# A depthwise convolution and a gated feed-forward: inputs cast to bf16 by POOL's DMA queue in place of fp32 tiles and casts on the engines

## The chip, the cores and the metric

The kernel runs on one core of a Trainium2 chip. The metric is device microseconds of one execution. The median of three runs of the kernel before is 559.08 us (558.78 to 559.87); the execution that was profiled took 559.35 us.

## What is computed

The input `x` has 8 sequences of 3904 rows with 192 values (fp32). Each of 8 heads (24 columns) has 7 taps; their softmax is a causal convolution along the sequence, and its result, 31232 rows of 192, goes through a gated feed-forward with `d_ff` = 1024:

```
out[b, s, h, :] = sum over k of softmax(weight[h])[k] * x_pad[b, s + k, h, :]
y  = out.reshape(31232, 192)
return ((y @ w1) * (y @ w2)) @ w3 @ w_out
```

All inputs and the output are fp32.

## The kernel before

**Layout.** The rows are cut into two streams of 15616 (`NS = 2`), which ride together: partitions 0 to 63 hold stream 0, 64 to 127 stream 1. The convolution works on windows of 64 rows (58 new ones and 6 of history); 272 windows a stream are grouped in ten blocks of 10, 10, 10, 30, 32 and five times 36 windows (`SIZES`). The feed-forward works on chunks of 512 rows a stream, 31 of them (`NR`), the last of 256.

**Convolution.** `load_x` (L91) brings a block's windows into fp32 tiles `xr` (two buffers; blocks 0 to 2 take one tile, the others two halves). The loads go out on SP's DMA queue, a few on ACT's; each is 64 partitions by so many windows of 192 values, so each contiguous run is 768 bytes. `cast_x` (L127) zeroes the history rows at the start of a sequence with memsets on POOL, waits for the loads and casts the tile to bf16 (`xb`, two buffers), on POOL but for half of block 0 (ACT). `conv` (L246) multiplies with a banded 64 x 64 matrix of taps (`Aband`, made by `band_taps` and `band_sum`, L216 to L230, from masks that POOL makes at L174) and evicts into `convo` on ACT and DVE. `store` (L277) writes `convo` to the scratch `rows` in DRAM by SP's queue; `transposes` (L316) brings it back by DMA transposes as `xT`, three tiles that hold a ring of four chunks. The first blocks go another way: `pe_transposes` (L301) makes `xT` on TensorE, with copies on DVE and ACT.

**Feed-forward.** `first_product` (L344) makes `pa` and `pb` for eight tiles `ft` of `d_ff`, with two sets of weights (`wn` as loaded, `wsw`, printed as `ws`, with the halves of 64 partitions swapped), ACT copies `pa` to `asb` and DVE multiplies into `abT`. The weights `w1`, `w2` are loaded as fp32 (`wf`, L160) in two halves of 512 columns; `cast_w` (L332) casts each half to `wn` on POOL and to `wsw` on DVE, ACT and POOL. `w3` and `w_out` are loaded by POOL's queue with the cast to bf16 on the way (L396, L400) and multiplied once into `W_sb` (L402 to L417). `second_product` (L369) multiplies `abT` with `W_sb`, ACT copies to `osb` (a ring of six `slot` buffers, which `wf` and the band's products share) and SP's queue writes the output.

**Order.** Nothing is rescheduled: each engine and each queue works in the order in which the program names its instructions. The prologue (L422 to L472) names loads, casts, first convolutions, chunks 0 to 2 of the first product with blocks 1 to 3 of the convolution between their tiles, and the product of `w3` and `w_out`. Then a loop over R (L484) takes in each round the first product of chunk R, the second of chunk R - 2, some heads of the next block's convolution (`plan`), after a block's last head its store and the cast of the next block, the transposes of chunk R + 2, and, where a block's first head was among the heads, the loads of the block after it.

Of the kernel before, what the change touches and what calls it, by code (L numbers as in the profile page):

```python
# [9 lines left out]
FP32 = mybir.dt.float32  # L10
BF16 = mybir.dt.bfloat16
# [6 lines left out]
def kernel(  # L18
# [10 lines left out]
    nc = tc.nc  # L29
# [6 lines left out]
    PAD = K - 1  # L36
# [35 lines left out]
        return psum.tile([128, 16, 128], BF16, tag="banks", name=name)  # L72

    def slot(shape, dtype, name):
        return stage.tile(shape, dtype, tag="slot", bufs=6, name=name)

    rows = dram.tile([TS, NP * NS * Q], BF16, name="rows")

# [3 lines left out]
        return [(FIRST[b], 2 * n)] if 2 * n <= MAXN else [(FIRST[b], n), (FIRST[b] + n, n)]  # L82

    x_rows = x.rearrange("b s d -> (b s) d")
    xr_of, xb_of, zero_rows = {}, {}, {}

    def x_window(r, i, m):
        return bass.AP(tensor=x.tensor, offset=(r * TS + tok(i) - PAD) * D,
                       ap=[[D, Q], [ST * D, m], [1, D]])

    def load_x(b, q1=nc.sync):  # L91
        tiles = []
        zeros_of = zero_rows[b] = []
        for i0, n in halves_of(b):
            xr = work.tile([128, n, D], FP32, tag="xr", bufs=2, name="xr")
            w = 0
            if i0 == 0:
                nc.gpsimd.memset(xr[0:32, 0, :], 0.0)
                for p0, p1 in ((PAD, PAD + 48), (PAD + 48, Q)):
                    nc.sync.dma_start(out=xr[p0:p1, 0, :], in_=x_rows[p0 - PAD:p1 - PAD, :])  # L100
                nc.sync.dma_start(out=xr[0:Q, 1:n, :], in_=x_window(0, 1, n - 1))
                q1.dma_start(out=xr[Q:128, :, :], in_=x_window(1, 0, n))
                zeros_of.append((xr, 1, 0))
                w = n
            while w < n:
                i = i0 + w
                m = min(n - w, WB - i % WB)
                at_end = i + m == NWIN
                if at_end:
                    m -= 1  # L110
                if m:
                    for r, q in ((0, nc.sync), (1, q1)):
                        q.dma_start(out=xr[Q * r:Q * r + Q, w:w + m, :], in_=x_window(r, i, m))
                if i % WB == 0:
                    zeros_of += [(xr, 0, w), (xr, 1, w)]
                w += m
                if at_end:
                    nc.gpsimd.memset(xr[Q:128, w, :], 0.0)
                    t = tok(NWIN - 1) - PAD
                    nc.sync.dma_start(out=xr[0:Q, w, :], in_=x_rows[t:t + Q, :])  # L120
                    nc.sync.dma_start(out=xr[Q:Q + PAD + LAST, w, :],
                                      in_=x_rows[TS + t:TS + t + PAD + LAST, :])
                    w += 1
            tiles.append(xr)
        xr_of[b] = tiles

    def cast_x(b, engines=None):  # L127
        tiles = []
        for xr, r, w in zero_rows.pop(b):
            nc.gpsimd.memset(xr[Q * r:Q * r + PAD, w, :], 0.0)  # L130
        for xr in xr_of.pop(b):
            n = xr.shape[1]
            xb = work.tile([128, n, D], BF16, tag="xb", bufs=2, name="xb")
            parts = engines or [nc.gpsimd.tensor_copy]
            step = -(-n // len(parts))
            for e, f in enumerate(parts):
                ws = slice(e * step, min(n, (e + 1) * step))
                f(out=xb[:, ws, :], in_=xr[:, ws, :])  # L138
            tiles.append(xb)
        if len(tiles) == 1:  # L140
            n = SIZES[b] // 2
            xb_of[b] = [(tiles[0], 0), (tiles[0], n)]
        else:
            xb_of[b] = [(tiles[0], 0), (tiles[1], 0)]


    wall = const.tile([128, H, K], FP32)
    nc.scalar.dma_start(out=wall, in_=weight.partition_broadcast(128))
    load_x(0, nc.scalar)

    tiny = const.tile([128, 1], FP32)
    nc.vector.memset(tiny, 0.0)
    zeros = const.tile([128, CH], BF16)
    nc.vector.memset(zeros, 0.0)  # L154
    nc.scalar.activation(out=tiny, in_=tiny, func=ACT.Exp)

    wf = [slot([128, DFF], FP32, f"wf{k}") for k in range(3)]
    HC = DFF // 2

    def load_w(half, q1):  # L160
        cs = slice(half * HC, (half + 1) * HC)
        nc.sync.dma_start(out=wf[0][:, cs], in_=moe_w1[0:128, cs])
        q1.dma_start(out=wf[1][:, cs], in_=moe_w2[0:128, cs])
        nc.sync.dma_start(out=wf[2][0:Q, cs], in_=moe_w1[128:192, cs])
        q1.dma_start(out=wf[2][Q:128, cs], in_=moe_w2[128:192, cs])

    load_w(0, nc.scalar)

    ones = const.tile([128, 1], BF16)
    nc.gpsimd.memset(ones, 1.0)  # L170
# [2 lines left out]
    for m, base in ((cmask, 0), (lmask, -Q)):  # L173
# [2 lines left out]
            pattern=[[-1, K], [-1, Q]], compare_op=ALU.is_equal,  # L176
            fill=0.0, base=base, channel_multiplier=1)
    nc.vector.tensor_copy(out=cmask[Q:128], in_=lmask[Q:128])
    ident = const.tile([128, 128], BF16)
    make_identity(nc, ident)  # L180

    def warm(n):
        t = banks("warm")
# [40 lines left out]
    def band_sum(g):  # L224
        with nc.allow_low_precision(reason="one tap and zeros"):
            nc.vector.reduce_sum(out=Aband[:, g, 0],
                                 in_=cprod_of.pop(g).rearrange("p h k s -> p h s k"),
                                 axis=AX.X)
        nc.vector.tensor_copy(out=Aband[Q:128, g, 1], in_=Aband[0:Q, g, 0])
        nc.scalar.copy(out=Aband[0:Q, g, 1], in_=Aband[Q:128, g, 0])  # L230
# [15 lines left out]
    def conv(b, h0, nh, evict=None):  # L246
        n = SIZES[b] // 2
        if h0 == 0:
            convo_of[b] = work.tile([128, n, NP, NS, Q], BF16, tag="convo", bufs=2, name="convo")
        convo = convo_of[b]  # L250
        cps = banks("cps")
        wd = nh * G

        def view(ps, r):
            return cps[ps, r, 0:n * wd].rearrange("p (w g) -> p w g", g=wd)

        for j in range(nh):
            h = h0 + j
            for c in range(2):
                xb, w0 = xb_of[b][c]  # L260
                for r in range(NS):
                    nc.tensor.matmul(  # L262
                        view(slice(Q * c, Q * c + Q), r)[:, :, j * G:(j + 1) * G],
                        band_of(h, r),
                        xb[Q * r:Q * r + Q, w0:w0 + n, h * G:(h + 1) * G],
                        start=True, stop=True)
        src = cps[:, :, 0:n * wd].rearrange("p r (w g) -> p r w g", g=wd)
        o = 0
        for e, (k, c0, m) in enumerate(segments(h0 * G, wd)):
            dst = convo[:, :, k, :, c0:c0 + m].rearrange("p w r g -> p r w g")  # L270
            f = evict or [nc.scalar.copy]
            f[e % len(f)](out=dst, in_=src[:, :, :, o:o + m])  # L272
            o += m
        if h0 + nh == H:
            del xb_of[b]
# [45 lines left out]
                out=xT[k][:, a:a + t1 - t0], in_=rows[t0:t1, k * 128:(k + 1) * 128])  # L321


    wn = [const.tile([128, DFF], BF16, name=f"wn{k}", tag=f"wn{k}") for k in range(3)]
    wsw = [const.tile([128, DFF], BF16, name=f"ws{k}", tag=f"ws{k}") for k in range(3)]

    def w_of(i, k, r):
        if k == 2:
            return (wn if i == r else wsw)[2]
        return (wn if k == r else wsw)[i]  # L330

    def cast_w(k, half, direct, swap):  # L332
        cs = slice(half * CH, (half + 1) * CH)
        direct(out=wn[k][:, cs], in_=wf[k][:, cs])
        for f, (d, s) in zip(swap, ((0, Q), (Q, 0))):
            f(out=wsw[k][d:d + Q, cs], in_=wf[k][s:s + Q, cs])  # L336


    abT_of = {}
# [79 lines left out]

    V, A, P = nc.vector.tensor_copy, nc.scalar.copy, nc.gpsimd.tensor_copy  # L420

    load_w(1, nc.sync)  # L422
    load_x(1)
    band_taps(0, nc.vector)
    band_taps(1, nc.gpsimd)
    cast_x(0, engines=(A, P))
    load_x(2, nc.scalar)
    band_sum(0)
    band_sum(1)
    conv(0, 0, 4)  # L430
    warm(3)
    cast_w(0, 0, P, (V, A))
    conv(0, 4, 4, evict=(V, A))
    cast_w(2, 0, P, (V, A))
    cast_w(1, 0, P, (P, P))
    pe_transposes(0)
    for k in (0, 2, 1):
        cast_w(k, 1, P, (P, A))
    cast_x(1)
    load_x(3)  # L440
    load_wo()
    for jt in range(2):
        load_w3(jt)
    cast_x(2)
    for jt in range(2, JT):
        load_w3(jt)

    def seq(*fs):
        def run():
# [6 lines left out]
        5: seq((conv, 1, 4, 4)),  # L456
        7: seq((pe_transposes, 1), (store, 1, 19), (conv, 2, 0, 4))})
    first_product(1, {
        0: seq((conv, 2, 4, 4), (cast_x, 3), (store, 2), (transposes, 2, 1152), (load_x, 4)),
        7: seq((conv, 3, 0, 1), (conv, 3, 1, 1))})  # L460
    first_product(2, {
        1: seq((conv, 3, 2, 1), (conv, 3, 3, 1)),
        3: seq((conv, 3, 4, 1), (conv, 3, 5, 1)),
        5: seq((conv, 3, 6, 1), (conv, 3, 7, 1), (store, 3), (transposes, 3), (transposes, 4))})

    cast_x(4)
    w3_transpose(0)
    w3_transpose(1)
    for jt in range(JT):
# [14 lines left out]
    for R in range(LAG, NR + LAG):  # L484
        if LAG < R < NR:
            first_product(R)
        for r in range(NS):
            second_product(R - LAG, r)
        heads = plan.get(R, [])
        for j, (b, h) in enumerate(heads):  # L490
            conv(b, h, 1, (V,) if j < 2 else (A,))
        if heads and heads[-1][1] == H - 1:
            store(b)
            if b + 1 < NB:
                cast_x(b + 1)
        if LAG < R < NR - 2:
            transposes(R + 2)
        if heads and heads[0][1] == 0 and b + 1 < NB:
            load_x(b + 1)


# [28 lines left out]
```

## Time and profile before

| what | value |
|---|---|
| profiled execution | 559.35 us |
| its span (first to last instruction of the profile) | 557.6 us |
| PE busy | 528.1 us (95%) |
| DVE, ACT, POOL busy | 356.3, 319.9, 64.5 us |
| SP's queue (q1) | 128294 packets, 73.16 MB |
| POOL's queue (q0) | 2192 packets, 2.49 MB |
| ACT's queue (q10) | 1680 packets, 1.41 MB |
| chain that ended last: PE, DMA, ACT, DVE | 87%, 5%, 3%, 2% |

How to read it: busy times are of one execution and overlap. The chain that ended last is followed back from the last instruction, at each step to what released it, and so says on what the end depended. A bracket behind a row of the timeline names the idle time of its engine before it and what ended it. "SPq" is SP's issuing of DMAs. Bytes are counted as written, so a cast from fp32 to bf16 counts half of what is read.

### The profile page before, as it was taken

How to read it: one execution, taken by the hardware profiler on the slowest of the kernel's cores; microseconds unless marked ns; L12 is line 12 of the kernel's file. 1: busy time of each engine (PE TensorE's matmuls, PEld its weight loads, DVE VectorE, ACT ScalarE, POOL GpSimd, SP SyncE). 2: the span in 40 equal slices, each digit the busy share in tenths (PEclk: the TensorE clock that was granted, in tenths of full speed). 3: DMA queues.
4: the chain of work that ended last, by engine and by line, in shares of the span. 5: the costliest groups of instructions: out<-in, count | busy, mean ns of one | idle time of the engine just before them, and what ended most of it. 6: DMA issues, size and time to landing. Idle time of an engine off the chain costs nothing.

```text
span 557.6 us, 12681 instructions
## 1 busy us (share of the span) xinstructions
PE 528.1 (95%) x5425; PEld 343.7 (62%) x5425; DVE 356.3 (64%) x329; ACT 319.9 (57%) x360; POOL 64.5 (12%) x56
## 2 busy tenths in 40 slices
PE   5892889999999999999999999999999999999997
PEld 2441367666566666566666666666655666665587
DVE  5573374667866667876666886666786655677640
ACT  2872645555665555665555665554666555566642
POOL 5733030013004000040000400021000000000000
PEclk8897799999999999999999999999999999999999
DMA  8898898957896899367982779827234462223214
GB/s 183 165 223 189 162 198 161 193 117 157 184 215 141 152 177 186 80 152 149 200 184 56 163 165 198 157 73 144 70 86 86 116 160 62 65 58 86 72 58 142
DMA packets 132222, 77.86 MB, mean 140 GB/s; under 512 B 49858, under 2 KB 130374, under 8 KB 132166
## 3 DMA queue, kind: packets, MB, share of 16 engines
q1 hardware_dynamic: 128294, 73.16, 62.3%
q0 software_dynamic: 2192, 2.49, 2.6%
q10 hardware_dynamic: 1680, 1.41, 1.2%
q8 instruction: 42, 0.69, 0.6%
q14 instruction: 14, 0.11, 0.1%
HBM read 33.29 MB, written 35.13 MB: 123 GB/s over the span
## 4 chain that ended last, share of the span: by engine, by line
PE 87%; DMA 5%; ACT 3%; DVE 2%; SPq 1%; issue 1%; ACTq 0%; POOL 0%; POOLq 0%
PE ops L375 28%; PE pa L357 28%; PE pb L357 27%; DMA xT<-rows 2%; PE cps L262 2%; ACT asb L363 2%; DMA xr<-in_x_dram 2%; DVE abT L364 1%; DMA rows<-convo 1%; PE wps L415 1%; ACT osb L380 1%; SPq L320 1%; PE w3ps L406 0%; PE tps L307 0%; ACT ws L336 0%
## 5 line engine op out<-in xcount | busy, mean ns | idle before, releaser
L364 DVE TENSOR_TENSOR abT<-asb,pb 128x1024 bf16<-128x1024 bf16 (+1 forms) x248 | 298.0, 1203 | 79.3 <-ACT asb L363 49.2
L363 ACT CAST asb<-pa 128x1024 bf16<-128x1024 f32 (+1 forms) x248 | 247.4, 999 | 75.0 <-PE pa L357 74.1
L357 PE MATMUL pa<-xT,wn 64*128 64x512 bf16 (+1 forms) x744 | 200.8, 374 | 4.9 <-DMA xT<-rows 1.4
L357 PE MATMUL pa<-xT,ws 64*128 64x512 bf16 (+1 forms) x744 | 200.9, 374 | 2.5 <-DMA xT<-rows 1.9
L357 PE MATMUL pb<-xT,wn 64*128 64x512 bf16 (+1 forms) x744 | 201.8, 374 | 0.7 <-DVE abT L364 0.7
L357 PE MATMUL pb<-xT,ws 64*128 64x512 bf16 (+1 forms) x744 | 195.3, 374 | 0.0
L357 PEld LDWEIGHTS <-wn 64*128 64x128 bf16 x1488 | 137.4, 94 | 91.5 <-issue 13.2
L357 PEld LDWEIGHTS <-ws 64*128 64x128 bf16 x1488 | 128.9, 94 | 74.0 <-issue 10.0
L375 PEld LDWEIGHTS <-abT 128*128 128x128 bf16 x1952 | 159.6, 98 | 11.7 <-issue 11.7
L375 PE MATMUL ops<-W_sb,abT 128*128 128x192 bf16 x1952 | 166.1, 246 | 0.0
L380 ACT COPY osb<-ops 128x768 f32<-128x768 f32 (+1 forms) x62 | 48.8, 788 | 127.7 <-PE ops L375 127.7
L272 DVE CAST convo<-cps 128x864 bf16<-128x864 f32 (+4 forms) x53 | 44.9, 894 | 95.4 <-PE cps L262 95.4
L138 POOL CAST xb<-xr 128x3456 bf16<-128x3456 f32 (+4 forms) x17 | 45.6, 2701 | 238.5 <-PE cps L262 155.5
L262 PE MATMUL cps<-xb,Aband 64*64 64x432 bf16 (+3 forms) x320 | 19.0, 320 | 15.2 <-POOL xb L138 9.9
L272 ACT CAST convo<-cps 128x640 bf16<-128x640 f32 (+8 forms) x29 | 15.3, 581 | 11.6 <-PE cps L262 10.7
L262 PEld LDWEIGHTS <-Aband 64*64 64x64 bf16 x320 | 6.5, 109 | 24.1 <-issue 21.4
L130 POOL MEMSET xr<- 6x192 f32 x7 | 1.7, 250 | 67.2 <-DMA xr<-in_x_dram 67.1
L185 PE MATMUL warm<-zeros 128*128 128x512 bf16 x19 | 8.0, 604 | 1.3 <-DVE zeros L154 1.3
L415 PE MATMUL wps<-wo_b,w3T 128*128 128x192 bf16 x64 | 6.6, 246 | 1.3 <-DVE w3T L409 1.2
L409 DVE COPY w3T<-w3ps 128x1024 bf16<-128x1024 bf16 x8 | 5.4, 689 | 2.9 <-PE w3ps L406 2.9
L417 ACT CAST W_sb<-wps 128x192 bf16<-128x192 f32 x8 | 2.5, 318 | 8.2 <-PE wps L415 8.2
L415 PEld LDWEIGHTS <-w3T 128*128 128x128 bf16 x64 | 5.1, 98 | 1.7 <-DVE w3T L409 1.7
(41 smaller groups left out, 50.9 us busy)
## 6 DMA issues: line engine op xcount, KB each, us to landing
out_dram<-osb SPq DMA_DIRECT2D x60, 384.0 KB
xr<-in_x_dram SPq DMA_DIRECT2D x14, 864.0 KB
rows<-convo SPq DMA_DIRECT2D x7, 648.0 KB
xr<-in_x_dram SPq DMA_DIRECT2D x4, 720.0 KB
xr<-in_x_dram SPq DMA_DIRECT2D x5, 480.0 KB
xr<-in_x_dram SPq DMA_DIRECT2D x6, 384.0 KB
w3b<-in_moe_w_dram POOLq DMA_DIRECT2D x8, 256.0 KB, 12.8
xr<-in_x_dram SPq DMA_DIRECT2D x2, 816.0 KB
```

The lines of the kernel that those rows point to most:

```text
L138: f(out=xb[:, ws, :], in_=xr[:, ws, :])
L185: nc.tensor.matmul(t[:, j % 2, :], zeros[:, 0:128], zeros, start=True, stop=True)
L262: nc.tensor.matmul(view(slice(Q * c, Q * c + Q), r)[:, :, j * G:(j + 1) * G], band_of(h, r), xb[Q * r:Q * r + Q, w0:w0 + n, h * G:(h + 1) ...
L272: f[e % len(f)](out=dst, in_=src[:, :, :, o:o + m])
L320: nc.sync.dma_start_transpose(out=xT[k][:, a:a + t1 - t0], in_=rows[t0:t1, k * 128:(k + 1) * 128])
L357: nc.tensor.matmul(p[:, r, 0:N], w_of(i, k, r)[rs, ft * 128:(ft + 1) * 128], xT[k][rs, r0:r0 + N], start=(k == 0), stop=(k == NP - 1))
L363: nc.scalar.copy(out=asb[:, :, 0:N], in_=pa[:, :, 0:N])
L364: nc.vector.tensor_tensor(out=ab[:, ft, :, 0:N], in0=asb[:, :, 0:N], in1=pb[:, :, 0:N], op=ALU.mult)
L375: nc.tensor.matmul(ops[:, g // 2, (g % 2) * D:(g % 2) * D + D], ab[:, jt, r, g * 128:(g + 1) * 128], W_sb[:, jt, :], start=(jt == 0), stop ...
L380: nc.scalar.copy(out=osb.rearrange("p (a g) d -> p a (g d)", g=2), in_=ops[:, 0:ng // 2, 0:2 * D])
L409: nc.vector.tensor_copy(out=w3T_of[jt], in_=tps[:, 0:JT, :])
L415: nc.tensor.matmul(wps[:, 0, 0:D], w3T[:, gt, :], wo_b[:, gt, :], start=(gt == 0), stop=(gt == JT - 1))
```

## The change

All of x and all weights of the first product go by POOL's queue (`nc.gpsimd.dma_start`) straight into bf16 tiles, the cast being made on the way. The fp32 tiles `xr` and `wf` and the casts `cast_x` and `cast_w` are gone; what stays of the latter is `swap_w`, which copies the halves of 64 partitions from `wn` to `wsw`. `xb` has six buffers in place of two, the `slot` ring five in place of six. The zero rows at the start of a sequence are set in `xb` just before the block's first convolution. In block 0 the first window is loaded apart (`load_first`), after the masks. Block 4 is loaded in the prologue after `w3`, and in the loop the next block's loads stand ahead of the heads of the block before.

```diff
     def slot(shape, dtype, name):
-        return stage.tile(shape, dtype, tag="slot", bufs=6, name=name)
+        return stage.tile(shape, dtype, tag="slot", bufs=5, name=name)
...
-    def load_x(b, q1=nc.sync):
+    def load_x(b):
...
-            xr = work.tile([128, n, D], FP32, tag="xr", bufs=2, name="xr")
+            xb = work.tile([128, n, D], BF16, tag="xb", bufs=6, name="xb")
...
+                nc.gpsimd.memset(xb[:, 0, :], 0.0)
+                for r in range(NS):
+                    nc.gpsimd.dma_start(out=xb[Q * r:Q * r + Q, 1:n, :], in_=x_spans(r, 1, n - 1))
...
-                    for r, q in ((0, nc.sync), (1, q1)):
-                        q.dma_start(out=xr[Q * r:Q * r + Q, w:w + m, :], in_=x_window(r, i, m))
+                    for r in range(NS):
+                        nc.gpsimd.dma_start(out=xb[Q * r:Q * r + Q, w:w + m, :],
+                                            in_=x_spans(r, i, m))
...
-    def cast_x(b, engines=None):
...
+    def load_first():
+        xb = xb_of[0][0][0]
+        for r in range(NS):
+            for p0, p1 in ((PAD, PAD + 48), (PAD + 48, Q)):
+                nc.gpsimd.dma_start(
+                    out=xb[Q * r + p0:Q * r + p1, 0, :],
+                    in_=x_rows[r * TS + p0 - PAD:r * TS + p1 - PAD, :])
...
-    load_x(0, nc.scalar)
+    load_x(0)
...
-    wf = [slot([128, DFF], FP32, f"wf{k}") for k in range(3)]
...
-    load_w(0, nc.scalar)
...
     nc.vector.tensor_copy(out=cmask[Q:128], in_=lmask[Q:128])
+    load_first()
     ident = const.tile([128, 128], BF16)
     make_identity(nc, ident)
+
+    wn = [const.tile([128, DFF], BF16, name=f"wn{k}", tag=f"wn{k}") for k in range(3)]
+    wsw = [const.tile([128, DFF], BF16, name=f"ws{k}", tag=f"ws{k}") for k in range(3)]
+    nc.gpsimd.dma_start(out=wn[0], in_=moe_w1[0:128, :])
+    nc.gpsimd.dma_start(out=wn[2][0:Q], in_=moe_w1[128:192, :])
+    nc.gpsimd.dma_start(out=wn[2][Q:128], in_=moe_w2[128:192, :])
...
-    def cast_w(k, half, direct, swap):
-        cs = slice(half * CH, (half + 1) * CH)
-        direct(out=wn[k][:, cs], in_=wf[k][:, cs])
-        for f, (d, s) in zip(swap, ((0, Q), (Q, 0))):
-            f(out=wsw[k][d:d + Q, cs], in_=wf[k][s:s + Q, cs])
+    def swap_w(k, half, engines):
+        cs = slice(half * HC, (half + 1) * HC)
+        for f, (d, e) in zip(engines, ((0, Q), (Q, 0))):
+            f(out=wsw[k][d:d + Q, cs], in_=wn[k][e:e + Q, cs])
...
-    load_w(1, nc.sync)
-    load_x(1)
     band_taps(0, nc.vector)
     band_taps(1, nc.gpsimd)
-    cast_x(0, engines=(A, P))
-    load_x(2, nc.scalar)
+    nc.gpsimd.dma_start(out=wn[1], in_=moe_w2[0:128, :])
+    for b in (1, 2):
+        load_x(b)
     band_sum(0)
+    conv(0, 0, 4)
     band_sum(1)
-    conv(0, 0, 4)
     warm(3)
-    cast_w(0, 0, P, (V, A))
+    swap_w(0, 0, (V, A))
     conv(0, 4, 4, evict=(V, A))
-    cast_w(2, 0, P, (V, A))
-    cast_w(1, 0, P, (P, P))
+    swap_w(2, 0, (V, A))
+    swap_w(1, 0, (V, A))
     pe_transposes(0)
     for k in (0, 2, 1):
-        cast_w(k, 1, P, (P, A))
-    cast_x(1)
+        swap_w(k, 1, (P, A))
     load_x(3)
     load_wo()
-    for jt in range(2):
+    for jt in range(JT):
         load_w3(jt)
-    cast_x(2)
-    for jt in range(2, JT):
-        load_w3(jt)
+    load_x(4)
...
-        0: seq((conv, 2, 4, 4), (cast_x, 3), (store, 2), (transposes, 2, 1152), (load_x, 4)),
+        0: seq((conv, 2, 4, 4), (store, 2), (transposes, 2, 1152)),
...
-    cast_x(4)
...
         heads = plan.get(R, [])
+        if heads and heads[0][1] == 0:
+            b = heads[0][0]
+            for xb, r, w in zero_rows.pop(b):
+                nc.gpsimd.memset(xb[Q * r:Q * r + PAD, w, :], 0.0)
+            if b + 1 < NB:
+                load_x(b + 1)
         for j, (b, h) in enumerate(heads):
             conv(b, h, 1, (V,) if j < 2 else (A,))
         if heads and heads[-1][1] == H - 1:
             store(b)
-            if b + 1 < NB:
-                cast_x(b + 1)
         if LAG < R < NR - 2:
             transposes(R + 2)
-        if heads and heads[0][1] == 0 and b + 1 < NB:
-            load_x(b + 1)
```

Each engine's own work keeps its order: PE's instructions are the same, one for one, in the same order as before.

More of the change, by code (lines that the diff above doesn't have):

```diff
@@ L84, with x_spans @@
     x_rows = x.rearrange("b s d -> (b s) d")
-    xr_of, xb_of, zero_rows = {}, {}, {}
-    def x_window(r, i, m):
+    xb_of, zero_rows = {}, {}
+    def x_spans(r, i, m):
         return bass.AP(tensor=x.tensor, offset=(r * TS + tok(i) - PAD) * D,
                        ap=[[D, Q], [ST * D, m], [1, D]])
-    def load_x(b, q1=nc.sync):
+    def load_x(b):
         tiles = []
@@ L94, in load_x @@
         for i0, n in halves_of(b):
-            xr = work.tile([128, n, D], FP32, tag="xr", bufs=2, name="xr")
+            xb = work.tile([128, n, D], BF16, tag="xb", bufs=6, name="xb")
             w = 0
             if i0 == 0:
[L98 to L103, printed above, removed]
+                nc.gpsimd.memset(xb[:, 0, :], 0.0)
+                for r in range(NS):
+                    nc.gpsimd.dma_start(out=xb[Q * r:Q * r + Q, 1:n, :], in_=x_spans(r, 1, n - 1))
                 w = n
@@ L111, in load_x @@
                 if m:
-                    for r, q in ((0, nc.sync), (1, q1)):
-                        q.dma_start(out=xr[Q * r:Q * r + Q, w:w + m, :], in_=x_window(r, i, m))
+                    for r in range(NS):
+                        nc.gpsimd.dma_start(out=xb[Q * r:Q * r + Q, w:w + m, :],
+                                            in_=x_spans(r, i, m))
                 if i % WB == 0:
-                    zeros_of += [(xr, 0, w), (xr, 1, w)]
+                    zeros_of += [(xb, 0, w), (xb, 1, w)]
@@ L116, in load_x @@
                 w += m
                 if at_end:
-                    nc.gpsimd.memset(xr[Q:128, w, :], 0.0)
+                    nc.gpsimd.memset(xb[Q:128, w, :], 0.0)
                     t = tok(NWIN - 1) - PAD
-                    nc.sync.dma_start(out=xr[0:Q, w, :], in_=x_rows[t:t + Q, :])
-                    nc.sync.dma_start(out=xr[Q:Q + PAD + LAST, w, :],
-                                      in_=x_rows[TS + t:TS + t + PAD + LAST, :])
+                    nc.gpsimd.dma_start(out=xb[0:Q, w, :], in_=x_rows[t:t + Q, :])
@@ L123, in load_x @@
+                    nc.gpsimd.dma_start(out=xb[Q:Q + PAD + LAST, w, :],
+                                        in_=x_rows[TS + t:TS + t + PAD + LAST, :])
                     w += 1
-            tiles.append(xr)
-        xr_of[b] = tiles
-    def cast_x(b, engines=None):
[L128 to L138, printed above, removed]
@@ L139, in cast_x @@
             tiles.append(xb)
         if len(tiles) == 1:
-            n = SIZES[b] // 2
-            xb_of[b] = [(tiles[0], 0), (tiles[0], n)]
+            xb_of[b] = [(tiles[0], 0), (tiles[0], SIZES[b] // 2)]
         else:
             xb_of[b] = [(tiles[0], 0), (tiles[1], 0)]
+    def load_first():
[5 more added lines that the diff above has]
+                    in_=x_rows[r * TS + p0 - PAD:r * TS + p1 - PAD, :])
@@ L155 @@
     nc.scalar.activation(out=tiny, in_=tiny, func=ACT.Exp)
-    wf = [slot([128, DFF], FP32, f"wf{k}") for k in range(3)]
[L158 to L165, printed above, removed]
-    load_w(0, nc.scalar)
     ones = const.tile([128, 1], BF16)
@@ L321, in transposes @@
                 out=xT[k][:, a:a + t1 - t0], in_=rows[t0:t1, k * 128:(k + 1) * 128])
-    wn = [const.tile([128, DFF], BF16, name=f"wn{k}", tag=f"wn{k}") for k in range(3)]
-    wsw = [const.tile([128, DFF], BF16, name=f"ws{k}", tag=f"ws{k}") for k in range(3)]
     def w_of(i, k, r):
@@ L330, in w_of @@
         return (wn if k == r else wsw)[i]
-    def cast_w(k, half, direct, swap):
-        cs = slice(half * CH, (half + 1) * CH)
-        direct(out=wn[k][:, cs], in_=wf[k][:, cs])
-        for f, (d, s) in zip(swap, ((0, Q), (Q, 0))):
-            f(out=wsw[k][d:d + Q, cs], in_=wf[k][s:s + Q, cs])
+    HC = DFF // 2
+    def swap_w(k, half, engines):
+        cs = slice(half * HC, (half + 1) * HC)
+        for f, (d, e) in zip(engines, ((0, Q), (Q, 0))):
+            f(out=wsw[k][d:d + Q, cs], in_=wn[k][e:e + Q, cs])
     abT_of = {}
```

## The prediction

> **What bounds the kernel now.** I read the busy rows first, then the chain of waits in order of time, then the timelines of SP, PE and POOL where that chain leaves TensorE, and last the DMA queues in the same stretch. Busy time by stretch (columns: stretch; PE, PEld, DVE, ACT, POOL busy, each with its count; granted clock; DMA share; GB/s):
> ```profile
> 45.00:50.00 5.00, 0.40 (x4) 0.11 (x3) 1.71 (x2) 0.53 (x1) 0.00 (x0) 0.83 1.11 221
> 50.00:55.00 5.00, 0.00 (x0) 0.00 (x0) 0.00 (x0) 0.00 (x0) 2.30 (x1) 0.50 0.62 144
> ...
> 250.00:300.00 50.00, 50.00 (x514) 32.27 (x511) 35.85 (x34) 29.42 (x32) 0.50 (x2) 1.00 0.80 159
> ```
> From 85 us on TensorE is the bound: it is busy 50.00 of 50, and all its waits after 85 us, by the table of waits, are 3.0 us for the transposes (1.6 on PE, 1.4 on PEld) and about 1 for ACT. There the change can win next to nothing. The one large hole is in the prologue, between the first product of chunk 1 and that of chunk 2. The chain of waits through it (start, us, what):
> ```profile
> 44.52 1.02 ACT asb L363
> ...
> 46.80 6.98 DMA rows<-convo
> ...
> 53.96 1.22 SPq L320
> 55.24 1.22 SPq L320
> 56.56 3.07 DMA xT<-rows
> ```
> The end waited for block 2's store to `rows` and for the DMA transposes behind it. Why was that store so late? SP's timeline (start, us, engine, line, operation):
> ```profile
> 24.65 11.00 SPq L113 DMA_DIRECT2D xr<-in_x_dram  x4
> 35.70 11.49 SPq L298 DMA_DIRECT2D rows<-convo  x6
> 53.96 4.27 SPq L320 DMA_TRANSPOSE xT<-rows  x3
> ```
> The four loads of block 3's x take SP 11.00 us to issue, 2.75 each, while the kernel's lone issues take 0.3 to 0.9. The store behind them takes 9.39 us (the longest L298 issue) to get in, and then queues in the same ring. Block 2's `convo` was ready at 36.8 (ACT's eviction, 35.80 for 1.02); its store landed at 53.8. A second gate stands beside it: conv of block 3 needs the last quarter of x and its cast on POOL.
> ```profile
> 52.70 2.59 POOL L138 CAST xb<-xr 128x2880 bf16<-128x2880 f32 x1 [9.27 <-DMA xr<-in_x_dram]
> ```
> ```profile
> 55.34 0.81 PE L262 MATMUL cps<-xb,Aband 64*64 64x360 bf16 x6 [9.94 <-POOL xb L138]
> 56.64 0.60 PE L357 MATMUL pa<-xT,wn 64*128 64x512 bf16 x1 [0.50 <-ACT convo L272]
> 56.65 0.61 PE L357 MATMUL pa<-xT,ws 64*128 64x512 bf16 x1
> 58.95 0.58 PE L357 MATMUL pa<-xT,ws 64*128 64x512 bf16 x1 [1.70 <-DMA xT<-rows]
> ```
> So chunk 2's product begins in earnest at 58.95, though PE had nothing left from 45.4 on. Whoever moves either gate alone meets the other: 55.3 by x, 58.95 by the transposes. The change moves both.
>
> **Part by part.** *SP's queue.* All of x and the weights leave it. In program order SP then begins with block 1's store, block 2's store and three transposes. Nothing holds them but their data.
>
> *Casts.* POOL loses 17 casts of x (45.6 us in all); the last gate loses 2.59 us. Elsewhere POOL is 12% busy and off the path: nothing. The six fp32 weight casts (`wn`) on POOL go as well. Of the swap copies (`ws`) ACT makes 6 for 5, DVE 3 for 2, POOL 3 for 5. ACT loses its half of the first cast of x (0.99).
>
> *POOL's own queue.* A POOL issue is shown by two rows, the second for two DMAs:
> ```profile
> 24.57 1.09 POOL L396 DMA_DIRECT2D wo_b<-in_moe_w_out_dram  x1
> 25.66 1.07 POOL L400 DMA_DIRECT2D w3b<-in_moe_w_dram  x2
> ```
> That is 1.09 us for 1024 rows and 0.53 for 128; 576 rows come between, 0.8. Before POOL's part of the band (L218, 2.59 us) now stand two such (1.6), four small ones (at most 0.53 each, 2.1) and three weight loads (1.6), beside the memsets, masks and identity that were there: 0.81 + 0.25 + 1.6 + 1.3 + 2.1 + 0.5 + 1.6 = 8.2, so the band part ends at 10.8 (before: 8.6) and `wn1` is issued by 11.3. Waiting on it is DVE's second band sum (1.69), then its copy and ACT's copy: the second conv starts near 13.0 instead of 14.7. In the first conv the wait for x goes: 10.88 for its landing and 1.00 for ACT's cast, after which ACT made the band copy at 12.62. Now x0 is 1268 packets alone in the ring, done near 8 to 9.5. `wn1` (128 packets of 4 KB, 1.2 us at 152 ns on 16 engines) should land at 14 to 15, just before DVE and ACT reach its swap; both stand in line there ahead of the copies to xT. I take the start as 1 us earlier; from 1.5 earlier to 7 later (a landing that takes 10.0 us, as `wo_b` did beside other traffic).
>
> *x by the software queue.* Packets by queue in two one-microsecond stretches, 28 to 29 (x by SP's ring, alone) and 30 to 31 (mostly `wo_b`, cast to bf16, same 768 B rows read; columns: packets, MB as written, share of 16 engines):
> ```profile
> q1 hardware_dynamic: 271, 0.21, 115.5%
> ```
> ```profile
> q0 software_dynamic: 369, 0.14, 134.0%
> q1 hardware_dynamic: 75, 0.05, 34.4%
> ```
> 271 packets a microsecond by the one, 444 with the other. Up to and with block 3 the new queue carries 7668 such packets and 384 of 4 KB (3.6 us): at 400 a microsecond 22.8 us of work, with start and gaps of POOL done near 31; at 271, near 38.5. Either is before 44, when conv of block 3 wants it. The x gate at 55.3 goes. Speaking against this is the Trainium skill, DMA: Bandwidth & Descriptors, Specifications: below 512 B an SDMA engine reads, modifies and writes, and x as bf16 lands in runs of 384 B. `wo_b` lands in 384 B runs too, and the row above shows no slowing; by the rule I would take the 271 pace, which still comes before 44.
>
> *Store and transposes, now beside another queue.* From 36 to 38, x3 on q1 against w3 (4 KB reads) on q0:
> ```profile
> q0 software_dynamic: 175, 0.32, 84.8%
> q1 hardware_dynamic: 174, 0.13, 26.4%
> ```
> One for one: beside w3, q1 gets 87 packets a microsecond. From 32 to 33, beside 768 B rows, it got 211. Block 2's store is 580 packets, the three transposes 1152 (384 rows each). Data ready at 35.8. Lower bound: four issues (1.6) and 580 at 271 (2.2), then 5.1 as now (53.83 to 58.95): 44.7. Upper bound: both wholly against w3, 6.6 + 13.2 and 2.5 of latencies: 58.1. By the 400 pace w3 fills the queue from about 33.5 to 45, so the store goes against w3 (to 44.3 with latency) and the transposes against x4 (1152 at 211, 5.5 us, and start-up): 50.5. I take 50.5: **8.45 us gained** on 58.95. PE itself is ready near 44.
>
> *What is late next.* POOL runs ahead: with six buffers, block 5's loads go out as soon as x4 is there and block 6's once conv of block 3 is done, about 62. They meet block 3's store (1740 packets) and six transposes, due at 90.55 - 8.45 = 82.1: 205 packets an engine for the first three, at 84 to 100 ns beside x, 17 to 20 us: 79 to 83 from 62 or 63. I charge 0.8, from 0 to 3. From 75.3 to 84.4 (w3) PE paces itself, and w3 is in by 55.
>
> *The loop.* Same PE order, PE full: 0, from 1 less (the two small transpose stalls near 187 and 386 follow a store, not a load of x) to 2 more (transposes beside x). The osb ring of 5 for 6: one osb per 2.65 us even at the end, so a slot comes back after 13 us: 0.
>
> **Sum.** The profiled execution took 559.35 (span 557.6 and 1.75 around it): 559.35 - 8.45 + 0.8 = 551.7. The median of the runs is 0.27 lower: **551.4**.
>
> **Rivals.**
> *Full cover* (0.15). If w3 has drained, or POOL issues it late, the store and transposes run free: chunk 2 starts at 44.7 to 47; 545 to 547.5. For it: 444 packets a microsecond. Against: q0 then has 11 MB to read (block 3's 2.95, `wo` and w3 5.0, block 4's 3.1) and no reason to pause.
> *The neighbour takes it back* (0.17). Both meet w3, or the loads that run ahead delay chunk 3's transposes: chunk 2 at 54 to 58, or 3 us later on: 555 to 560. This holds the case that nothing is seen (0.07). For it: the one-for-one rows.
> *Slower: POOL's issue* (0.17). Ten DMAs and the band part stand ahead of `wn1`, and behind `wn1` the swaps, the copies to xT, and all PE work. If an issue costs c, the other work ahead being 0.81 + 0.25 + 1.3 + 0.5 + 2.6 = 5.5, `wn1` lands at 5.5 + 10c + 3, and swap and copies to xT (1.5) let the product start at 10 + 10c, for 18.6 now (the first product's second group): late by 10c - 8.6. The hole hides 14.5 of that (58.95 - 44.4), so it decides from c = 2.3 on. The rows say 0.53 to 1.09; SP paid 2.75 where its ring was full. At 2.75: 18.9 late, 4.4 past the cover, 563.8, and more where two such waits add.
> *As forecast* (0.51): 547.5 to 555.
>
> The range is 545 to 560; the slower case is left out. About 0.2% (1.1 us) is what a measurement here tells from none. Faster 0.51 + 0.15 + 0.10 = 0.76, same 0.07, slower 0.17.
>
> **What would show it.** SP's block 2 store issued near 36 with no 9 us issue; the rows<-convo landing near 44, xT near 50; PE's hole from 44 to about 50 and not 59; conv of block 3 not waiting for x; the loop unchanged at 16.4 us a round. Wrong would be: POOL issues over 1.5 us; `wn1` landing after 20; PE waiting for xT at chunk 3; or rounds longer than 16.5.

## The result, and the profile after

The changed kernel takes 586.84 us (median of 4 runs, 585.55 to 589.23) against 559.12 for the kernel before on the same chip (4 runs, 558.78 to 559.87): a ratio of 1.0499, with a 95% interval from 1.0463 to 1.0535. It is 5% slower; 551.4 was forecast. The profiled execution took 585.55 us, 26.2 more than that of before, and its span of 583.8 us is 26.2 longer too, so the whole loss lies in the span. In the rows PE is TensorE, ACT ScalarE, DVE VectorE and POOL GpSimd.

First the page's row on the chain that ended last, and its rows of 40 slices for PE and its granted clock (busy share and clock in tenths):

```profile
PE 80%; DMA 12%; ACT 3%; POOL 2%; DVE 2%; SPq 1%; issue 1%; ACTq 0%; POOLq 0%
```
```profile
PE   6894888996999689997899989999999999999997
...
PEclk8996998999899989999799999999999999999999
```
DMA's share of the chain went from 5% to 12%, and PE's from 87% to 80%. PE has dips in slices 4 to 7, in slices 10, 14 and 19, counted from 1. The clock is lower in slices 4 and 7 and in the slice after each of the last three dips. A slice is 14.6 us, so those three lie near 140, 195 and 270 us. The hole was to be in the prologue alone; there are three new ones in the loop, where the kernel before had PE busy throughout.

The prologue itself did much of what was foreseen. Busy time by stretch (same columns as above), around the old hole and in the loop:

```profile
45.00:50.00 5.00, 0.00 (x0) 0.00 (x0) 0.00 (x0) 0.13 (x1) 2.38 (x5) 0.86 1.54 182
50.00:55.00 5.00, 2.53 (x12) 0.79 (x14) 0.00 (x0) 0.67 (x1) 1.52 (x2) 0.50 1.86 166
85.00:90.00 5.00, 1.58 (x18) 0.52 (x12) 1.82 (x2) 1.47 (x3) 0.00 (x0) 0.95 1.33 124
250.00:300.00 50.00, 43.80 (x434) 28.58 (x432) 27.84 (x25) 23.00 (x24) 4.75 (x7) 0.93 0.72 126
```
PE comes back in 50 to 55, where it had nothing before; but it is idle most of 85 to 90, and from 250 to 300 it is busy 43.80 of 50 where it was busy 50.00. The chain of waits, from its stretches 40 to 60, 64 to 95 and 120 to 160 (start, us, what):

```profile
42.69 1.02 ACT asb L346
...
45.15 7.88 DMA xT<-rows
53.07 0.61 PE pa L340 x2
54.30 1.28 PE pb L340 x6
```
```profile
67.53 7.71 DMA rows<-convo
75.30 1.87 SPq L305
77.21 1.50 SPq L305
78.75 10.90 DMA xT<-rows
90.30 1.28 PE pb L340 x6
```
```profile
134.50 2.76 PE ops L358 x32
137.37 9.35 DMA xT<-rows
146.76 0.61 PE pa L340 x2
147.36 1.28 PE pb L340 x6
148.64 1.28 PE pa L340 x6
149.92 1.23 PE pb L340 x6
151.15 0.65 PE pa L340 x6
```
Chunk 2 gets its first `pb` group at 54.30 for 60.29 before: 6.0 us won. Chunk 3 waits for block 3's store and transposes, 7.71 and 10.90 us on their way, and all is lost again: the second product that follows chunk 3's first product starts at 101.39, for 101.09 before. Then a wait comes once a block. The third fence shows the second cost of each: after the idle time the next three groups of six matmuls take 1.28, 1.28 and 1.23 us instead of 0.65; the granted clock was 0.50 from 146 to 151 us and 1.00 from 151 to 156. The same `pa` group that begins at 151.15 here begins at 143.29 before, and the run came into this stretch 0.25 late: 7.6 us lost, some 5.8 by the wait and 1.85 by the slow groups.

Laid side by side, the starts of the rounds' second products give the account of the loop (us; rounds left out between the rows):

| start before | start after | late by |
|---|---|---|
| 134.25 | 134.50 | 0.25 |
| 151.06 | 158.92 | 7.86 |
| 184.29 | 192.15 | 7.86 |
| 201.79 | 217.84 | 16.05 |
| 234.75 | 250.81 | 16.06 |
| 267.57 | 292.33 | 24.76 |
| 316.94 | 341.70 | 24.76 |
| 333.36 | 359.78 | 26.42 |
| 540.78 | 566.66 | 25.88 |

Three steps of 7.6, 8.2 and 8.7, and between them nothing. After them the run loses 1.7 more and gets 0.5 back, with no x under way; why is not shown. What stands beside the three steps? POOL's timeline, the loads of blocks 6 to 9, with the idle time before them and what ended it:

```profile
66.44 4.50 POOL L110 DMA_DIRECT2D xb<-in_x_dram  x6 [14.92 <-PE cps L247]
...
124.56 3.40 POOL L110 DMA_DIRECT2D xb<-in_x_dram  x4 [44.00 <-issue]
...
181.91 4.52 POOL L110 DMA_DIRECT2D xb<-in_x_dram  x6 [53.95 <-PE cps L247]
...
257.21 3.44 POOL L110 DMA_DIRECT2D xb<-in_x_dram  x4 [58.55 <-issue]
```
And SP's timeline, at the first and second of these:

```profile
67.16 6.02 SPq L283 DMA_DIRECT2D rows<-convo  x4
75.30 12.31 SPq L305 DMA_TRANSPOSE xT<-rows  x6
```
```profile
126.99 3.47 SPq L283 DMA_DIRECT2D rows<-convo  x4
131.78 7.58 SPq L305 DMA_TRANSPOSE xT<-rows  x3
```
Block 6's x goes out at 66.44, and block 3's store at 67.16; block 7's x goes out at 124.56, and the store's larger part at 126.99 with the transposes behind it. This is no chance. In the loop POOL has little to do but these loads, so it comes to them long before their place in the program and stands at the wait for a buffer. With six buffers (a block takes two tiles) x of block b + 1 is released by the last convolution matmul of block b - 2, and that is the event after which SP stores block b - 2 and issues the transposes that a coming chunk needs. For blocks 6 and 8 the rows name it ("PE cps L247"). For blocks 7 and 9 the profile shows no releaser ("issue"), and the buffer count says it; for block 7 the chain of waits has those matmuls just before 124.56:

```profile
123.58 0.45 PE cps L247 x8
```
So the loads of all four blocks start together with a store and its transposes.

Packets by queue in two microseconds of these transposes (q0 is POOL's queue, q1 SP's; packets, MB as written, share of 16 engines), first after (142 to 144), then before (144 to 146), where nothing else was on the way:

```profile
q0 software_dynamic: 551, 0.21, 87.9%
q1 hardware_dynamic: 524, 0.13, 57.4%
```
```profile
q1 hardware_dynamic: 916, 0.22, 49.1%
```
Where both have work, the two queues share the engines one packet for one, and the transposes fall from 458 packets a microsecond (with the engines idle for part of that time) to 262. The Trainium skill (DMA: Bandwidth & Descriptors, Queues, rings and completion order) says that each engine goes round the queues that have work, packet by packet; the two rows above agree, 551 to 524. In the kernel before x stood in the same queue as these transposes and behind them, and could take nothing from them. SP's timeline there:

```profile
140.99 3.86 SPq L320 DMA_TRANSPOSE xT<-rows  x3
144.94 8.72 SPq L113 DMA_DIRECT2D xr<-in_x_dram  x6
```

### The profile page after: what moved, and what is told of

Read it like the earlier page. It is cut to its first block, busy times and chain, and to the rows that moved or that the text cites. A ratio compares the mean times of both kernels' runs of the same rounds, so it can differ in the third digit from the quotient of the medians.

```text
span 583.8 us, 12613 instructions
## 1 busy us (share of the span) xinstructions
PE 535.8 (92%) x5425; PEld 343.8 (59%) x5425; DVE 358.4 (61%) x330; ACT 319.6 (55%) x360; POOL 50.1 (9%) x80
## 4 chain that ended last, share of the span: by engine, by line
PE 80%; DMA 12%; ACT 3%; POOL 2%; DVE 2%; SPq 1%; issue 1%; ACTq 0%; POOLq 0%
PE pa L340 27%; PE pb L340 27%; PE ops L358 25%; DMA xT<-rows 10%; PE cps L247 1%; ACT asb L346 1%; DMA rows<-convo 1%; DVE abT L347 1%; DMA wn<-in_moe_w_dram 1%; SPq L305 1%; ACT convo L257 0%; POOL xb L133 0%; ACT osb L363 0%; POOL xb L100 0%; ACT ws L319 0%
## 5 line engine op out<-in xcount | busy, mean ns | idle before, releaser
L340 PE MATMUL pa<-xT,wn 64*128 64x512 bf16 (+1 forms) x744 | 206.6, 381 | 24.2 <-DMA xT<-rows 21.5
L340 PE MATMUL pa<-xT,ws 64*128 64x512 bf16 (+1 forms) x744 | 206.7, 381 | 11.3 <-DMA xT<-rows 10.6
L340 PEld LDWEIGHTS <-wn 64*128 64x128 bf16 x1488 | 138.8, 95 | 119.9 <-issue 26.3
L340 PE MATMUL pb<-xT,wn 64*128 64x512 bf16 (+1 forms) x744 | 206.2, 380 | 0.7 <-DVE abT L347 0.7
L340 PE MATMUL pb<-xT,ws 64*128 64x512 bf16 (+1 forms) x744 | 199.8, 381 | 0.0
L340 PEld LDWEIGHTS <-ws 64*128 64x128 bf16 x1488 | 130.9, 95 | 82.0 <-issue 19.3
L110 POOL DMA_DIRECT2D xb<-in_x_dram x38 | 29.9, 809 | 175.6 <-issue 103.1
L247 PE MATMUL cps<-xb,Aband 64*64 64x432 bf16 (+3 forms) x320 | 18.9, 322 | 5.2 <-DVE Aband L211 2.9
L247 PEld LDWEIGHTS <-Aband 64*64 64x64 bf16 x320 | 6.4, 110 | 14.5 <-issue 8.2
L170 PE MATMUL warm<-zeros 128*128 128x512 bf16 x19 | 6.5, 507 | 1.3 <-DVE zeros L144 1.3
L383 POOL DMA_DIRECT2D w3b<-in_moe_w_dram x8 | 4.3, 558 | 7.9 <-DMA xb<-in_x_dram 6.7
```

The lines of the kernel that those rows point to most:

```text
L110: nc.gpsimd.dma_start(out=xb[Q * r:Q * r + Q, w:w + m, :], in_=x_spans(r, i, m))
L170: nc.tensor.matmul(t[:, j % 2, :], zeros[:, 0:128], zeros, start=True, stop=True)
L247: nc.tensor.matmul(view(slice(Q * c, Q * c + Q), r)[:, :, j * G:(j + 1) * G], band_of(h, r), xb[Q * r:Q * r + Q, w0:w0 + n, h * G:(h + 1) ...
L340: nc.tensor.matmul(p[:, r, 0:N], w_of(i, k, r)[rs, ft * 128:(ft + 1) * 128], xT[k][rs, r0:r0 + N], start=(k == 0), stop=(k == NP - 1))
```

## The experiments

The theory: **POOL's queue runs ahead, and x meets the store and the transposes that are awaited.** Its first rival: the loop's loss is the price of x coming by a second queue with a cast, whenever it comes (packets of 384 bytes written). Its second: the loads are merely named too early, ahead of the heads. Its third: six buffers are what lets them collide, and fewer would hold them back.

**The loads held behind the transposes.** A copy of one element of `xT` by POOL waits for the transposes of chunk R + 2 and stands in POOL's order ahead of the loads:

```diff
+    seen = const.tile([1, 1], BF16, name="seen", tag="seen")
...
+    def gate(R):
+        a = (R * CH) % RING
+        nc.gpsimd.tensor_copy(out=seen, in_=xT[2][0:1, a:a + 1])
...
-            if b + 1 < NB:
-                load_x(b + 1)
...
+        if heads and heads[0][1] == 0 and b + 1 < NB:
+            gate(R + 2)
+            load_x(b + 1)
```

> The changed kernel, but the loads of blocks 5 to 9 are named at the end of the round in which the block before has its first head, behind that round's transposes, and a one-element copy on POOL that reads the last transpose's output stands ahead of them, so POOL cannot run ahead: x starts only when the transposes have landed. Theory collision (x, released by a block's last conv, shares the 16 engines one for one with that block's store and the transposes that chunk last + 3 waits for): the four holes of 6 to 10 us at 85, 137, 195 and 268 close and block 5 no longer lies beside chunk 2's transposes, so 585.6 - 6 - 7.6 - 8.2 - 8.7 - 1 to 3 = 552 to 554, and the hole before chunk 2 is 1 to 3 us shorter. Rival software queue (casting DMAs or their descriptors slow whatever runs, at any time): the time stays above 575. Rival buffers or slot ring: 585.

Measured: 553.17 (552.1 to 554.1), ratio 0.9887 (0.9865 to 0.991). All 33.7 us come from when five blocks' loads run. The first rival falls: the loads are the same, with the same cast and queue. One part of the expectation failed: the hole before chunk 2 is no shorter, though block 5's loads no longer lie there (the transposes end at 53.26, for 53.03 in the changed kernel).

**Block 4 as well.** Its loads go from the prologue's end behind the gate of chunk 2's transposes, behind the first tile of chunk 1's first product:

```diff
-    def gate(R):
-        a = (R * CH) % RING
+    def gate(R, first=0):
+        a = max(R * CH, first) % RING
...
-    load_x(4)
...
-        0: seq((conv, 2, 4, 4), (store, 2), (transposes, 2, 1152)),
+        0: seq((conv, 2, 4, 4), (store, 2), (transposes, 2, 1152), (gate, 2, 1152), (load_x, 4)),
```

> As the one before, and block 4's load as well waits behind the transposes of chunk 2. Theory collision: the transposes of chunk 2, which were issued at 43.9 and moved nothing until 48 while block 4's x ran, land 3 to 5 us sooner; chunk 2's product starts near 48 to 49 instead of 53; 547 to 551. Rival software queue: as the kernel before this one, within 1 us.

Measured: 547.78 (547.41 to 547.94), ratio 0.9791 (0.9769 to 0.9812). The chain of waits at chunk 2's transposes, first with the loop's loads alone held back, then with block 4's too:

```profile
45.44 7.82 DMA xT<-rows
```
```profile
45.46 3.09 DMA xT<-rows
```
The transposes land 4.7 us earlier, most of the 5.4 by which the time fell. POOL's timeline in the second of these kernels shows the gate and what it costs (0.18 us), at a round in the loop:

```profile
136.47 0.18 POOL L326 COPY seen<-xT 1x1 bf16<-1x1 bf16 x1 [53.54 <-DMA xT<-rows]
...
136.92 4.49 POOL L110 DMA_DIRECT2D xb<-in_x_dram  x6 [0.28 <-PE pa L346]
```

**No late loads at all.** The loads and zero rows of blocks 6 to 9 are left out, and these blocks work on block 5's x, so that part of the work is not done.

```diff
     def load_x(b):
+        if b > 5:
+            xb_of[b], zero_rows[b] = xb_of[5], []
+            return
...
-        if h0 + nh == H:
+        if h0 + nh == H and b < 5:
             del xb_of[b]
```

> The changed kernel without the loads and zero rows of blocks 6 to 9: these blocks convolve block 5's tiles again, so that part of the computation is left out. Theory collision: the holes at 85, 137, 195 and 268 close, 553 to 557. Rivals that blame something other than x traffic in the loop (the slot ring of five, the weights, the clock): 580 or more.

Measured: 554.78 (one run). With the loads gone the time is that of the kernel with the loads held back, within 2 us; from the second product near 129 us to the last one the run takes 406.4 us without the loads and 404.8 with them held back. So x by POOL's queue costs the loop nothing that shows if it comes at the right moment, and the collision is the loss.

**Only the place in the program.** The loop's loads are named where the first experiment names them, at the round's end, but without the gate:

```diff
-            if b + 1 < NB:
-                load_x(b + 1)
...
+        if heads and heads[0][1] == 0 and b + 1 < NB:
+            load_x(b + 1)
```

> The changed kernel with the loop's loads only named later, at the end of the round, behind the transposes, as in the kernel before; no wait is added. Theory collision by release: POOL's queue holds nothing else, so the place in the program does nothing and the release by the last conv three blocks before decides; loads at 66, 124, 182 and 257 as before, the same four holes, 586 with 3 us either way. Rival (the order in the program is what counts): 553, as with the wait.

Measured: 587.51 (585.31 to 588.44), ratio 1.0497 (1.0465 to 1.053), the same as the change. POOL's timeline shows why (four groups of its rows):

```profile
65.10 4.48 POOL L110 DMA_DIRECT2D xb<-in_x_dram  x6 [13.11 <-PE cps L247]
...
124.16 3.39 POOL L110 DMA_DIRECT2D xb<-in_x_dram  x4 [44.98 <-issue]
...
182.45 4.51 POOL L110 DMA_DIRECT2D xb<-in_x_dram  x6 [54.90 <-PE cps L247]
...
257.44 3.44 POOL L110 DMA_DIRECT2D xb<-in_x_dram  x4 [58.27 <-issue]
```
The loads go out where they did, within 1.4 us. POOL has little else to do here, so the place in the program sets no time; the wait alone does. The second rival falls.

**Four buffers for six.**

```diff
-            xb = work.tile([128, n, D], BF16, tag="xb", bufs=6, name="xb")
+            xb = work.tile([128, n, D], BF16, tag="xb", bufs=4, name="xb")
```

> The changed kernel with four buffers of x instead of six. Block b + 1's tiles are then released by the last conv of block b - 1, not b - 2: block 5's load starts with block 3's store, block 6's with block 4's, and so on to block 9's with block 7's, five collisions for four. Theory: the hole near 345 grows from 1.7 to 6 to 10 us and the others stay, 590 to 595. Rival (more traffic ahead of time is what hurts, fewer buffers help): below 585.

Measured: 600.35 (one run), slower as expected, and by more than expected. Now x of block b + 1 is released one block later, by the last convolution matmul of block b - 1, and again that is the event of a store. Each block's loads meet the store after the one that they met before, so there is one collision more: block 9's loads and the chain, near 340 us.

```profile
335.98 3.44 POOL L110 DMA_DIRECT2D xb<-in_x_dram  x4 [62.69 <-PE cps L247]
```
```profile
348.85 13.06 DMA xT<-rows
```
With six buffers the transposes near 345 took 4.52 us. The last second product starts 14.8 us later than with six (581.47 for 566.66), and 10.9 of that come here. The third rival falls: with four as with six buffers the load is tied to the end of some block's convolution, and so to a store. Other counts were not tried.

**The queue alone, in the kernel before.** There the five loop loads, fp32 and without a cast, go by POOL's queue instead of SP's, those of the last window too; nothing else is changed.

```diff
-    def load_x(b, q1=nc.sync):
+    def load_x(b, q1=nc.sync, q0=nc.sync):
...
-                    for r, q in ((0, nc.sync), (1, q1)):
+                    for r, q in ((0, q0), (1, q1)):
...
-            load_x(b + 1)
+            load_x(b + 1, nc.gpsimd, nc.gpsimd)
```

> The kernel before, with one thing changed: the fp32 loads of blocks 5 to 9 go by POOL's queue instead of SP's; no cast on the way, same tiles, same POOL casts. POOL's next load is then held only by its own cast, and that by the last conv two blocks before. Theory collision: the loads of blocks 6 to 9 start with a store and its transposes as in the changed kernel; four holes of 6 to 10 us and 0 to 5 near 85: 583 to 604. Rival (the cast on the way, or rows of 384 bytes): within 4 us of 559.

Measured: 653.49 (one run), 94 us above the kernel before on that chip (559.55). The chain has five holes, one a block:

```profile
81.94 21.98 DMA xT<-rows
...
145.91 25.44 DMA xT<-rows
...
215.34 27.12 DMA xT<-rows
...
302.42 25.78 DMA xT<-rows
...
388.46 27.05 DMA xT<-rows
```
The direction was expected, the size was not. Packets by queue from 156 to 160 show it:

```profile
q0 software_dynamic: 167, 0.65, 97.1%
q1 hardware_dynamic: 166, 0.04, 6.9%
```
Again one for one, 167 to 166. But here POOL's queue makes packets of 3.9 KB of its 768-byte rows (0.65 MB by 167), and the transposes get 42 packets a microsecond; beside x with the cast they got 262, and alone 458. Neither the cast nor the six buffers are needed for the loss: the move to POOL's queue is enough, and in these two cases the larger packets are the worse. Whether ACT's queue would do the same was not tried.

**The same with the gate.** The gate is that of the first experiment.

```diff
+            gate(R + 2)
             load_x(b + 1, nc.gpsimd, nc.gpsimd)
```

> As p1 (the kernel before, blocks 5 to 9 loaded as fp32 by POOL's queue), with the same one-element copy ahead of each block's loads, so that they wait for the round's transposes. Theory: with the order back, queue and packet size do no harm; the five holes of 22 to 27 us of p1 close, 557 to 563. Rival (the POOL queue itself disturbs, or its large packets do at any time): above 575.

Measured: 558.68 (one run), with 560.72 for the kernel before on that chip. All 94 us are given back by the order alone, in a kernel that has none of the rest of the change. Each of the two kernels ran once, but 94 us lie far outside the spread of any kernel here.

**Two more steps on the good version.** First, the last four loads of `w3` also go behind the gate of chunk 2, since the transposes there still met them:

```diff
-    for jt in range(JT):
+    for jt in range(4):
         load_w3(jt)
...
-        0: seq((conv, 2, 4, 4), (store, 2), (transposes, 2, 1152), (gate, 2, 1152), (load_x, 4)),
+        0: seq((conv, 2, 4, 4), (store, 2), (transposes, 2, 1152), (gate, 2, 1152),
+               *[(load_w3, jt) for jt in range(4, JT)], (load_x, 4)),
```

> As g2, with the last four loads of w3 as well behind the transposes of chunk 2. Block 2's store then no longer shares the engines one for one with 4 KB reads (190 packets of each in 38 to 40) and lands 2 to 4 us sooner; the hole before chunk 2, 44 to 48.5 in g2, shrinks by as much; 544 to 546.5. Against: w3 and block 4's x move to 46 to 62 and may meet block 3's store at 62 or come late for the product of w3 at 65; then 548 to 551.

Measured: 543.02 (542.38 to 543.5), ratio 0.9707 (0.9684 to 0.973), a little better than expected. Busy time by stretch over the old hole:

```profile
40.00:45.00 5.00, 5.00 (x48) 2.58 (x44) 4.76 (x5) 3.87 (x5) 0.00 (x0) 1.00 0.26 59
45.00:50.00 5.00, 4.55 (x48) 1.94 (x48) 3.81 (x4) 4.88 (x8) 4.03 (x8) 1.00 0.56 94
```
The hole of the prologue is gone: PE works on at full clock, 4.55 of 5 us from 45 to 50, where the kernel before had 0.40 and then nothing. On the page PE has 90% of the chain and DMA 2%.

Second, POOL's part of the band (`band_taps(1)`) goes to DVE behind the first band sum, in the version before that (blocks 4 to 9 held back, `w3` not):

```diff
-    band_taps(1, nc.gpsimd)
...
     band_sum(0)
+    band_taps(1, nc.vector)
```

> As g2, but the second half of the band's taps is made on DVE, behind the first band sum, so nothing of POOL's stands between the weight loads. In g2 DVE's small copy at 9.23 took 1.80 us where it takes 0.19 in the kernel before; POOL's multiply ran for just those 1.8 us. Theory (the copy is held while POOL's instruction has the port that both share): the copy takes 0.19 again, the first conv starts 1.6 us sooner, wn1 is issued 1.7 us sooner; the first product starts 0.5 to 1.5 us sooner, of which the hole at 44 keeps some: 546 to 547.8. Rival (the copy waits for its own input): it stays 1.80, and 547.8.

Measured: 547.33 (544.49 to 549.51), ratio 0.9779 (0.9732 to 0.9827): not to be told from the version without it. DVE's copy of the band, first without, then with the edit:

```profile
9.21 1.79 DVE L214 COPY Aband<-Aband 64x128 bf16<-64x128 bf16 x1
```
```profile
9.18 0.19 DVE L214 COPY Aband<-Aband 64x128 bf16<-64x128 bf16 x1
```
The copy is nine times shorter, but `wn1` lands near 15.1 in both (its transfer now takes from 9.15 to 15.16 where it took from 10.83 to 15.03; why it is longer is not shown), and the swaps behind it wait for that.

Both together:

> g3 and g4 together. Theory: chunk 2 has no hole left in g3, so whatever the first product gains at the start counts in full; but in g4 wn1 landed no earlier (15.2 against 15.1) because block 1's x lay beside it, so 0 to 1 less than g3: 542 to 543.

Measured: 542.16 (541.65 to 543.15), ratio 0.9672 (0.9656 to 0.9688), as expected. The interval overlaps that of the step with `w3` alone (0.9684 to 0.973) by a hair. Either of the two beats the kernel before by about 3% and the change by some 7.5%.

## Why the prediction was wrong, step by step

- **The loop, "0, from 1 less ... to 2 more (transposes beside x)": the step that failed.** It gave the transposes beside x 2 us at most for the whole loop and worked this out from no row. The runs showed 25.6 us: the second products are 0.30 late behind chunk 3 and 25.88 at the end, and 24.5 of that come in three steps, at the loads of blocks 7, 8 and 9. The prediction saw that POOL runs ahead for blocks 5 and 6, and did not carry that to blocks 7 to 9. It also had the price in hand, one packet for one, and used it in the prologue only. Its rival "the neighbour takes it back" named the mechanism, but paid for it once and not once a block.
- **What is late next, 0.8 us: mis-sized.** Measured 6.3 (6.0 gained at chunk 2, 0.3 late behind chunk 3). The prediction had block 6's x meet block 3's store and transposes, and took 17 to 20 us from 62 or 63 on for the store and the first three transposes. Block 6's x was issued at 66.44, four microseconds later than reckoned (conv of block 3 ended later), and these transposes landed at 89.65, 23.2 us behind it.
- **SP's queue freed: right.** Block 2's store has no 9 us issue any more (0.3 to 0.4 us each), and the transposes behind it are issued at 43.88, for a landing near 44 forecast. But the store, issued from 35.02 on, moved no packet until 38.5, beside `w3` on POOL's queue; the prediction had no such wait.
- **The transposes of chunk 2: right in kind, 2.5 us off.** They landed at 53.0 for 50.5, and 6.0 us were gained for 8.45. They were issued from 43.88 on, but moved 6 packets until 48, while POOL's queue moved 1014 packets from 44 to 46 and 987 from 46 to 48. With block 4's x and the last of `w3` held back, the hole is gone altogether, and the time of 543.02 is below the 545 of the forecast's own best case.
- **The gate of x: right.** Block 3's convolution found its x. In 44 to 46 the new queue moved 507 packets a microsecond for 271 by SP's ring; 400 was taken. The 384-byte runs cost nothing that shows.
- **The start: 1 us earlier taken, 1.8 measured**, a little outside its range (the second group of the first product at 16.82 for 18.59). `wn1` was issued at 10.85 to 11.49 (11.3 forecast), by luck in part: POOL's part of the band began at 9.21 for 8.2 and took 1.75 us for 2.59.
- **The slower rival, POOL's issue: wrong.** An issue costs 0.53 to 0.97 us; the rival needed 2.3.
- **The five `osb` slots, and PE's own work: no cost seen.** Between the steps the rounds are as long as before.

Taken together: with the run-ahead in the loop held back, the kernel runs at 553.17. The forecast without its 0.8 for the neighbour is 550.6, and with the 2.5 us by which chunk 2's transposes came late 553.1, within the spread of that kernel's runs (552.1 to 554.1). So the working was near in all but the one thing that decided; that the sum fits so closely is luck in part, since smaller terms were off both ways.

## What to carry to other kernels

When a load moves to an engine that has little else to do, ask what event releases its buffer, and what else that event starts: in this kernel that, and not its place in the program, set when the load ran. A load that stood behind an awaited transfer in one queue was held back by that queue; on POOL's queue it took packet for packet from it, so put the order back, for example with a one-element copy that reads the awaited data (0.18 us on POOL, worth 34 us here and 95 in the other kernel). A price found at one block is to be multiplied by the number of blocks before it is called small.

## What the runs showed of the hardware

- **Sharing is by packets, not by bytes.** The transposes' packets are of about 240 to 250 bytes (0.22 MB by 916, 0.13 MB by 524), and their pace hangs on the packets of the other queue: 458 a microsecond alone, 262 beside 384-byte packets, 42 beside 3.9 KB ones. POOL's queue gathers 768-byte rows into such large packets without the cast, and with it makes a packet of each row (551 packets, 0.21 MB).
- **A wait costs more than its length.** After the wait for the transposes that took 9.35 us from 137.37 on, three groups took 1.28, 1.28 and 1.23 us instead of 0.65, at a granted clock of 0.50: 1.85 us on top.
- **DVE's small copy waited for POOL.** Beside POOL's multiply (9.21 to 10.96) a copy that takes 0.19 us alone took 1.80 and ended at 11.03. The Trainium skill (SBUF — State Buffer, Who interferes with whom) says that the two share a pair of ports, which DVE takes in some modes that a copy can run in, and which the first to issue holds for a whole instruction; the copy's 0.19 once POOL's multiply was away agrees. No run shows in which mode the copy ran.
- **Left open: a late start beside a busy POOL queue.** The transposes issued at 43.88 moved almost nothing for four microseconds, and block 2's store nothing for 3.5, while POOL's queue was busy. With block 4's x held back, the transposes issued at 42.87 moved 741 packets from 44 to 46, and in the kernel before those issued at 53.96 started within 1.5 us. That is about 2.6 us more than alone for the transposes (an estimate: 4.0 less 1.4), as much as they came late by the forecast. No run tells why.
